# DMA transposes of x in two parts: a fused attention and MLP kernel

## The chip, the cores and the metric

One core of a Trainium2 chip runs the whole kernel. The metric is the device time of one execution in microseconds; the time of a kernel is the median over its runs.

## The reference

Eight batches of eight heads attend from 576 queries to keys and values that are averaged over groups of 8 positions (72 pooled positions). The heads are put side by side, which gives x with 4608 tokens (8 batches of 576) and 512 columns. Two matrix products with a pointwise function between them follow:

```
k_p = k.reshape(B, H, 72, 8, 64).mean(axis=3);  v_p likewise
attn = softmax(q @ k_p.T / 8);  x = (attn @ v_p), heads side by side
h = x @ w_in            # 4608 x 512 by 512 x 2048
g = h - tanh(h)
out = g @ w_out         # 4608 x 2048 by 2048 x 512
```

## The kernel before

All orders are written out by hand; no scheduler moves anything. Tokens are worked in nine groups of 512 (`TG`), while attention makes x in batches of 576 (`S`). Batch b starts at token 576 b and group g at 512 g, so a batch runs ahead of its group: batch g + 1, made during group g, holds tokens for group g + 1 and, more of them from batch to batch, for group g + 2. A batch comes in five blocks: four of 128 tokens and one of 64.

A start-up part makes batch 0, batch 1 and the first group. From then on each group g (loop at L931, g = 1 to 8) has two phases:

- The input phase: `h_pair` and `h_one` multiply xT, the transposed x, by w_in (`h_mms`, L530), ACT makes the tanh (L542), DVE subtracts (L543) into Gt. Among these stand the preparations for batch g + 1 and g + 2: `k_dma_transpose` (L332) turns the pooled keys kd into kT by a DMA, `k_place` on GpSimd puts them where the scores read them, `store_tile` (L607) stores the previous group's output, ACT casts the raw queries to q_bf in three parts (`q_cast_part`, L192 and L197), `q_dma_transpose` (L205) turns them into qT in five blocks, and then the raw k, v and q of batch g + 2 are loaded (L137, L146, L141, L170, L162).
- The output phase: the product with w_out, done by a Strassen scheme in two by two blocks, seven products in 14 half steps u (`product`, L586). Between the half steps stand the scores of batch g + 1 (u = 0 to 4, L349) and its five blocks of the product with v (`av`, at u = 6, 7, 8, 9 and 11, L396). DVE divides each block by its sum (L413, L414) into an x_sb tile, of which there are five, one for each block in turn. At u = 6 GpSimd begins to pool the keys and values of batch g + 2 (`pool_k`, `pool_v`; the pooled keys kd are done with L256).

`av` ends each block, from g = 1 on, with a DMA transpose (L434), which writes the block's columns into xT, a ring of three groups' tokens (`RING` = 1536). A block that crosses the ring's end is turned in two pieces, which is the case of block 1 of batch 5.

All DMA transposes and all loads of the loop are issued by SP, one after the other in program order. The stores of the loop are issued by GpSimd. For each group the order on SP is: kT, five qT, seven loads, then the five blocks of x.

Of the kernel before, what the change touches and what calls it, by code (L numbers as in the profile page):

```python
# [15 lines left out]
B, H, S, D = 8, 8, 576, 64  # L16
# [10 lines left out]
TG = 512  # L27
# [7 lines left out]
RING = 3 * TG  # L35
# [7 lines left out]
def kernel(  # L43
# [9 lines left out]
    nc = tc.nc  # L53
# [44 lines left out]
    xT = const.tile([128, NFB, RING], BF16, name="xT")  # L98
# [51 lines left out]
    def load_k(b):  # L150
        return [
            load_main(k_pairs, k_raw[b % 2], b, 0, NM),
            load_dense(k_pairs, k_raw[b % 2], b),
        ]

    def load_v(b):
        return [load_main(v_pairs, v_raw[b % 2], b, 0, NM)] + load_left(
            v_pairs, v_raw[b % 2], b
        )
# [29 lines left out]
    def q_cast_part(b, n):  # L189
        t = q_raws[b]  # L190
        if n < 2:
            nc.scalar.copy(  # L192
                out=q_bf[:, 2 * n : 2 * n + 2, :, :].rearrange("p j h d -> p h j d"),
                in_=t[:, :, 2 * n : 2 * n + 2, :],
            )
        else:
            nc.scalar.copy(out=q_bf[:QT, R, :, :], in_=q_raws.pop(b)[:QT, :, R, :])  # L197

    def q_dma_transpose(b, j0=0, j1=R + 1):
        if j0 == 0:  # L200
            qTs[b] = work.tile([128, NHP, S], BF16, name="qT", tag="qT")
        qT = qTs[b]
        for j in range(j0, j1):
            rows = 128 if j < R else QT
            nc.sync.dma_start_transpose(  # L205
                out=qT[:, :, j * 128 : j * 128 + rows],
                in_=q_bf[:rows, j, :, :].rearrange("p h d -> p (h d)"),
            )
# [121 lines left out]
    def k_dma_transpose(b):  # L330
        kT = work.tile([128, NT, 128], BF16, name="kT", tag="kT", bufs=1)
        nc.sync.dma_start_transpose(  # L332
            out=kT[:, :, :], in_=kdups.pop(b)[:, :, :, :].rearrange("p t a d -> p (t a d)")
        )
        kTs[b] = kT

    def k_place(b, eng):
        kT = kTs.pop(b)
        kb_main(KB[b % 2], kT[:, 0:NM, :], 0, NM, (eng, eng))
        kb_left(KB[b % 2], kT[:, NM, :], eng)  # L340
# [68 lines left out]
    def av_half(b, blk, half, x_sb, alloc):  # L409
        ps = alloc([128, 4, D1], FP32, "x_ps")  # L410
        av_mms(b, blk, half, ps)
        rden = work.tile([128, 4, 1], FP32, name="rden", tag="rden", bufs=4)
        nc.vector.reciprocal(out=rden[:, :, :], in_=ps[:, :, D:D1])  # L413
        nc.vector.tensor_tensor(  # L414
            out=x_sb[:, half, :, :],
            in0=ps[:, :, 0:D],
            in1=rden[:, :, :].to_broadcast([128, 4, D]),
            op=ALU.mult,
        )

    def new_x():
        return work.tile([128, 2, 4, D], BF16, name="x_sb", tag="x_sb", bufs=5)

    def av(b, blk, alloc, by_dma):
        x_sb = new_x()
        for half in range(2):
            av_half(b, blk, half, x_sb, alloc)
        if by_dma:
            p0 = 0 if blk < 4 else 64
            pos = (b * S + blk * 128) % RING  # L430
            p1 = min(128, p0 + RING - pos)
            for r0, r1, c in ((p0, p1, pos), (p1, 128, 0)):
                if r1 > r0:
                    nc.sync.dma_start_transpose(  # L434
                        out=xT[:, :, c : c + r1 - r0],
                        in_=x_sb[r0:r1, :, :, :].rearrange("p a h d -> p (a h d)"),
                    )
        return x_sb

    def x_pe_transpose(b, blk, x_sb, fbs=(0, 4)):  # L440
        p0 = 0 if blk < 4 else 64
        pos = b * S + blk * 128
        f0, f1 = fbs
        xf = x_sb.rearrange("p a h d -> p (a h d)")
        ps = ps_any([128, f1 - f0, 128], FP32, "xT_ps")
        for fb in range(f0, f1):
            nc.tensor.matmul(
                ps[:, fb - f0, p0:128],
                lhsT=xf[:, fb * 128 : (fb + 1) * 128],
                rhs=ident[:, p0:128],  # L450
                start=True,
                stop=True,
            )
        nc.scalar.copy(out=xT[:, f0:f1, pos : pos + 128 - p0], in_=ps[:, :, p0:128])
# [83 lines left out]
    def h_pair(g, p, b0, ts):  # L538
        h_mms(g, p, PS[:, b0, :])
        h_mms(g, p + NP, PS[:, b0 + 1, :])  # L540
        t2 = TS[:, 2 * ts : 2 * ts + 2, :]
        nc.scalar.activation(out=t2, in_=PS[:, b0 : b0 + 2, :], func=ACT.Tanh)  # L542
        nc.vector.tensor_sub(out=Gt[:, p, :, :], in0=PS[:, b0 : b0 + 2, :], in1=t2)  # L543

    def h_one(g, p, s, b0, ts):
        h_mms(g, p + s * NP, PS[:, b0, :])
        nc.scalar.activation(out=TS[:, ts, :], in_=PS[:, b0, :], func=ACT.Tanh)
        nc.vector.tensor_sub(out=Gt[:, p, s, :], in0=PS[:, b0, :], in1=TS[:, ts, :])  # L548

    def sum_p(a, b):  # L550
        nc.vector.tensor_tensor(  # L551
            out=P[:, a:b, :], in0=Gt[:, a:b, 0, :], in1=Gt[:, a:b, 1, :], op=ALU.add
        )

    def sum_q(a, b):
        nc.vector.tensor_tensor(
            out=Q[:, a:b, :], in0=Gt[:, a:b, 0, 0:HT], in1=Gt[:, a:b, 1, HT:TG], op=ALU.add
        )
# [9 lines left out]
    def w_sum(out, a, b, op, eng=nc.vector, k0=0, k1=NP):  # L568
        return eng.tensor_tensor(  # L569
            out=out[:, k0:k1, :], in0=a[:, k0:k1, :], in1=b[:, k0:k1, :], op=op  # L570
        )
# [33 lines left out]
    def store_tile(g, tb):  # L605
        for r0, r1, dst in out_segments(g * TG + tb * 128, 128):
            nc.gpsimd.dma_start(out=dst, in_=O[r0:r1, tb, :])  # L607
# [102 lines left out]
    for m, base, step, cm in (  # L710
# [6 lines left out]
            out=m,  # L717
            in_=m,
# [6 lines left out]
    for i in range(2):  # L725
# [4 lines left out]
        out=spread.rearrange("p (t x) -> p t x", x=32)[:, :, 0:LO],  # L730
        in_=ident[:, 0 : NM * LO].rearrange("p (x t) -> p t x", t=NM),
# [156 lines left out]
    for u in range(16):  # L888
# [28 lines left out]
        if u in (9, 11):  # L917
            n = (u - 9) // 2
            nc.scalar.mul(
                out=w2s[:, 4, 4 * n : 4 * n + 4, :], in_=b22[:, 4 * n : 4 * n + 4, :], mul=-1.0  # L920
# [10 lines left out]
    for g in range(1, NG):  # L931
        nb = g + 1 if g + 1 < B else None
        nn = g + 2 if g + 2 < B else None
        for p in range(NP - 1):
            c = p if g > 1 else p - 1
            if nb is not None and 0 <= c < 3:
                q_cast_part(nb, c)
            h_pair(g, p, (0, 2, 4, 6, 0, 2, 4)[p], p % 2)
            if g == 1 and p < 4:
                w_sum(w2s[:, 0, :, :], b11, b22, ALU.add, k0=2 * p, k1=2 * p + 2)  # L940
            if 3 <= p < 6:
                sum_p(2 * p - 6, 2 * p - 4)
            if nb is not None and p == 0:
                k_dma_transpose(nb)
                k_place(nb, nc.gpsimd.tensor_copy)
            if g > 1 and p == 0:
                for tb in range(4):
                    store_tile(g - 1, tb)
            if nb is not None and 0 <= c < 3:
                q_dma_transpose(nb, 2 * c, min(2 * c + 2, R + 1))  # L950
            if nb is not None and c == 2:
                if nn is not None:
                    load_k(nn)
                    load_v(nn)
                    load_q(nn)
        h_one(g, NP - 1, 1, 0, 2)
        h_one(g, NP - 1, 0, 1, 3)
        sum_p(6, 8)
        sum_q(0, 4)
        sum_q(4, 8)  # L960
        ps_a = Banks(2, 3, 4, 5, 0, 1)
        for u in range(14):
            n, half = u // 2, u % 2
            bk, lhs, rhs = products[n]
            if n == 6 and g == NG - 1:
                break
            product(g, bk, lhs, rhs, 4 * half, 4 * half + 4, n < 2)
            if half:
                after_product(g, n)
                if g == 1 and n in (1, 2):  # L970
                    w_sum(w2s[:, 2, :, :], b21, b22, ALU.add, k0=4 * n - 4, k1=4 * n)
            if nb is not None:
                if u < NT:
                    scores(nb, u)
                if u == NT:
                    ps_a.n += 2
                if u in (6, 7, 8, 9, 11):
                    av(nb, (6, 7, 8, 9, 11).index(u), ps_b1, True)
                if u == 6 and nn is not None:
                    pool_k(nn, nc.gpsimd)  # L980
                    pool_v(nn, nc.gpsimd)
        if g < NG - 1:
            nc.scalar.copy(out=O[:, 0:2, 0:HD], in_=chain(g, C1))  # L983
# [43 lines left out]
```

## Time and profile before

| what | value |
|---|---|
| runs, us | 298.24, 305.23, 305.66, 307.6, 300.93 |
| median, us | 305.23 |
| profiled execution, us | 298.24, of which the span 296.5 |
| PE, DVE, ACT, POOL busy | 94%, 77%, 52%, 49% of the span |
| DMA queue of SP and its share of the 16 engines' time | 54,736 packets, 35.6 MB, 50.2% |
| chain that ended last | PE 67%, DMA 16%, DVE 6%, POOL 4% |
| xT transposes | 31, landing 2.7 us after issue (median), 6.4 us at most |
| loads of k, v, q (1 MB each) | 9.1, 11.1 and 11.3 us from issue to landing |

The span is the time from the first to the last instruction of the profiled execution; the run's own time is 1.7 us longer. In the timeline, times are microseconds from the span's start. Group g's input phase starts at 55.97 (g = 1), 87.19, 117.17, 147.08, 176.57, 205.79, 235.46 and 261.54 (g = 8). On SP a line's duration is the time that the issue takes, not the transfer; the landing is told separately.

### The profile page before, as it was taken

How to read it: one execution, taken by the hardware profiler on the slowest of the kernel's cores; microseconds unless marked ns; L12 is line 12 of the kernel's file. 1: busy time of each engine (PE TensorE's matmuls, PEld its weight loads, DVE VectorE, ACT ScalarE, POOL GpSimd, SP SyncE). 2: the span in 40 equal slices, each digit the busy share in tenths (PEclk: the TensorE clock that was granted, in tenths of full speed). 3: DMA queues.
4: the chain of work that ended last, by engine and by line, in shares of the span. 5: the costliest groups of instructions: out<-in, count | busy, mean ns of one | idle time of the engine just before them, and what ended most of it. 6: DMA issues, size and time to landing. Idle time of an engine off the chain costs nothing.

```text
span 296.5 us, 5447 instructions
## 1 busy us (share of the span) xinstructions
PE 279.5 (94%) x2021; PEld 178.6 (60%) x2040; DVE 227.3 (77%) x400; ACT 153.8 (52%) x244; POOL 145.0 (49%) x166
## 2 busy tenths in 40 slices
PE   7899989999989999999999999999999999999980
PEld 2454445445864587458745874588458845854870
DVE  5658675799986987598859895989698769838940
ACT  4647586586327642764276527652765155136310
POOL 8500819970399439923993299329931040130020
PEclk9999999999999999999999999999999999999996
DMA  7999999938734999599949995999460450030014
GB/s 255 221 213 280 316 217 316 282 78 290 192 71 86 252 332 141 99 228 328 146 86 246 308 149 100 268 328 122 76 180 2 80 142 2 0 130 13 0 30 114
DMA packets 64587, 49.85 MB, mean 168 GB/s; under 512 B 39984, under 2 KB 53296, under 8 KB 64560
## 3 DMA queue, kind: packets, MB, share of 16 engines
q1 hardware_dynamic: 54736, 35.60, 50.2%
q0 software_dynamic: 7248, 12.06, 18.6%
q10 hardware_dynamic: 2576, 1.84, 2.2%
q8 instruction: 16, 0.26, 0.4%
q14 instruction: 11, 0.09, 0.1%
HBM read 36.70 MB, written 9.44 MB: 156 GB/s over the span
## 4 chain that ended last, share of the span: by engine, by line
PE 67%; DMA 16%; DVE 6%; POOL 4%; SPq 2%; issue 1%; ACT 1%; ACTq 0%; POOLq 0%
PE PS L530 30%; PE PS L586 26%; DMA w1b<-in_moe_w_in_dram 4%; PE PS L512 4%; DMA k_raw<-in_k_dram 4%; DMA xT<-x_sb 3%; PE PS L396 3%; DMA v_raw<-in_v_dram 3%; PE PS L349 3%; DVE Gt L543 3%; DMA qT<-q_bf 2%; POOL k_raw L248 1%; SPq L137 1%; DVE w2s L569 1%; ACT TS L542 1%
## 5 line engine op out<-in xcount | busy, mean ns | idle before, releaser
L530 PE MATMUL PS<-xT,w1b 128*128 128x512 bf16 x496 | 111.1, 379 | 3.5 <-DMA xT<-x_sb 1.8
L543 DVE TENSOR_TENSOR Gt<-PS,TS 128x1024 bf16<-128x1024 f32 x56 | 68.4, 1221 | 29.2 <-ACT TS L542 29.2
L530 PEld LDWEIGHTS <-w1b 128*128 128x128 f16 x512 | 49.7, 98 | 62.6 <-issue 2.2
L542 ACT ACTIVATE TS<-PS 128x1024 f32<-128x1024 f32 x56 | 57.4, 1025 | 33.1 <-PE PS L530 27.7
L631 POOL TENSOR_TENSOR m<-O,m 128x512 f32<-128x512 f32 x8 | 11.5, 1435 | 95.7 <-ACT m L630 64.9
L414 DVE TENSOR_TENSOR x_sb<-PS,rden 128x256 bf16<-128x256 f32 x72 | 30.6, 425 | 2.5
L586 PE MATMUL PS<-w2s,Dg 128*128 128x256 f16 x256 | 30.2, 272 | 0.0
L607 POOL DMA_DIRECT2D out_dram<-O x44 | 23.6, 546 | 13.4 <-ACT O L983 13.4
L248 POOL TENSOR_TENSOR k_raw<-k_raw 128x512 f32<-128x512 f32 (+2 forms) x13 | 21.6, 1675 | 17.0 <-DMA k_raw<-in_k_dram 17.0
L586 PEld LDWEIGHTS <-Gt 128*128 128x128 bf16 x256 | 24.5, 98 | 5.9 <-DVE Gt L548 0.5
L586 PEld LDWEIGHTS <-P 128*128 128x128 bf16 x256 | 24.6, 98 | 4.7 <-issue 1.4
L586 PEld LDWEIGHTS <-Dg 128*128 128x128 bf16 x256 | 24.6, 98 | 2.8 <-issue 0.2
L368 ACT ACTIVATE E<-PS 128x288 bf16<-128x288 f32 x60 | 21.4, 410 | 7.9 <-PE PS L349 7.8
L551 DVE TENSOR_TENSOR P<-Gt 128x1024 bf16<-128x1024 bf16 x32 | 22.0, 687 | 0.6
L561 DVE TENSOR_TENSOR Dg<-Gt 128x1024 bf16<-128x1024 bf16 x32 | 21.1, 717 | 0.0
L396 PE MATMUL PS<-VB,E 128*128 128x130 bf16 x240 | 20.2, 220 | 0.1
L637 ACT COPY m<-PS 128x512 f32<-128x512 f32 x8 | 4.7, 586 | 29.5 <-PE PS L586 29.5
L267 POOL TENSOR_TENSOR v_raw<-v_raw 128x512 f32<-128x512 f32 (+1 forms) x12 | 19.2, 1620 | 0.0
L396 PEld LDWEIGHTS <-E 128*128 128x128 bf16 x240 | 16.8, 98 | 1.9 <-issue 0.4
L349 PE MATMUL PS<-qT,KB 128*128 128x288 bf16 (+5 forms) x128 | 17.3, 289 | 0.5 <-DMA qT<-q_bf 0.3
L586 PE MATMUL PS<-w2s,Gt 128*128 128x256 f16 x128 | 16.7, 273 | 0.4 <-DVE Gt L548 0.2
L983 ACT COPY O<-PS 128x512 f32<-128x512 f32 x7 | 4.1, 586 | 24.5 <-PE PS L586 24.5
(109 smaller groups left out, 399.1 us busy)
## 6 DMA issues: line engine op xcount, KB each, us to landing
k_raw<-in_k_dram SPq DMA_DIRECT2D x7, 1024.0 KB, 9.1
q_raw<-in_q_dram SPq DMA_DIRECT2D x7, 1024.0 KB, 11.3
v_raw<-in_v_dram SPq DMA_DIRECT2D x7, 1024.0 KB, 11.1
out_dram<-O POOLq DMA_DIRECT2D x32, 128.0 KB, 3.9
out_dram<-O POOLq DMA_DIRECT2D x12, 256.0 KB, 3.7
w1b<-in_moe_w_in_dram POOLq DMA_DIRECT2D x4, 512.0 KB, 14.1
w2b<-in_moe_w_out_dram POOLq DMA_DIRECT2D x4, 512.0 KB, 16.6
out_dram<-O SPq DMA_DIRECT2D x4, 256.0 KB, 4.2
```

The lines of the kernel that those rows point to most:

```text
L248: first = eng.tensor_tensor(out=r[:, ta:tb, 0:4, :], in0=r[:, ta:tb, 0:4, :], in1=r[:, ta:tb, 4:8, :], op=ALU.add)
L349: nc.tensor.matmul(dst[p : p + w], lhsT=KB[b % 2][:, o : o + w], rhs=qTs[b][:, m, c0:c1], start=True, stop=True,)
L368: nc.scalar.activation(out=E[:, t, half * hs : (half + 1) * hs], in_=ps[:, :], func=ACT.Exp, scale=SCALE)
L396: nc.tensor.matmul(ps[:, 2 * n : 2 * n + 2, :].rearrange("p h d -> p (h d)") if n < 2 else ps.rearrange("p (a s) d -> p a s d", s=2)[:, :, ...
L414: nc.vector.tensor_tensor(out=x_sb[:, half, :, :], in0=ps[:, :, 0:D], in1=rden[:, :, :].to_broadcast([128, 4, D]), op=ALU.mult,)
L530: nc.tensor.matmul(dst, lhsT=w1b[:, fb, i * 128 : (i + 1) * 128], rhs=xT[:, fb, c0 : c0 + TG], start=(fb == 0), stop=(fb == NFB - 1),)
L542: nc.scalar.activation(out=t2, in_=PS[:, b0 : b0 + 2, :], func=ACT.Tanh)
L543: nc.vector.tensor_sub(out=Gt[:, p, :, :], in0=PS[:, b0 : b0 + 2, :], in1=t2)
L551: nc.vector.tensor_tensor(out=P[:, a:b, :], in0=Gt[:, a:b, 0, :], in1=Gt[:, a:b, 1, :], op=ALU.add)
L561: nc.vector.tensor_tensor(out=Dg[:, a:b, :, :], in0=Gt[:, a:b, :, 0:HT], in1=Gt[:, a:b, :, HT:TG], op=ALU.subtract,)
L586: nc.tensor.matmul(part(g, bk, tt), lhsT=lhs(k, slice(tt * 128, (tt + 1) * 128)), rhs=rhs[:, k, :], start=(first and k == 0 and (tt == 0 o ...
L607: nc.gpsimd.dma_start(out=dst, in_=O[r0:r1, tb, :])
```

## The change

The blocks of batch b that group b does not read (first token at or after 512 (b + 1)) are no longer turned by `av`. They are put on a list, and the list is emptied in the next group, at the begin of its output phase, ahead of the products. In SP's order, these transposes then stand behind the next group's kT, qT and loads, and ahead of that group's own blocks of x. For batches 2 and 3 these are blocks 3 and 4, for batches 4 and 5 blocks 2 to 4, for batches 6 and 7 blocks 1 to 4.

```diff
         if by_dma:
-            p0 = 0 if blk < 4 else 64
-            pos = (b * S + blk * 128) % RING
-            p1 = min(128, p0 + RING - pos)
-            for r0, r1, c in ((p0, p1, pos), (p1, 128, 0)):
-                if r1 > r0:
-                    nc.sync.dma_start_transpose(
-                        out=xT[:, :, c : c + r1 - r0],
-                        in_=x_sb[r0:r1, :, :, :].rearrange("p a h d -> p (a h d)"),
-                    )
+            if b * S + blk * 128 < (b + 1) * TG:
+                x_dma_transpose(b, blk, x_sb)
+            else:
+                late.append((b, blk, x_sb))
         return x_sb
+
+    late = []
+
+    def x_dma_transpose(b, blk, x_sb):
+        p0 = 0 if blk < 4 else 64
+        pos = (b * S + blk * 128) % RING
+        p1 = min(128, p0 + RING - pos)
+        for r0, r1, c in ((p0, p1, pos), (p1, 128, 0)):
+            if r1 > r0:
+                nc.sync.dma_start_transpose(
+                    out=xT[:, :, c : c + r1 - r0],
+                    in_=x_sb[r0:r1, :, :, :].rearrange("p a h d -> p (a h d)"),
+                )
...
         sum_p(6, 8)
         sum_q(0, 4)
         sum_q(4, 8)
+        while late:
+            x_dma_transpose(*late.pop(0))
         ps_a = Banks(2, 3, 4, 5, 0, 1)
```

## The prediction

> **What bounds the kernel now.** I read the page first, then busy times by group, the waits of PE and its weight loads, and the timeline of SP's queue. The profiled run took 298.24 us (span 296.5 plus 1.7 around it), the lowest of the five shown; their median is 305.23. About 2% of it, 6.1 us, is what a measurement of this kernel can tell from no change, so the bounds are 299.1 and 311.3.
>
> ```profile
> span 296.5 us, 5447 instructions
> PE 279.5 (94%) x2021; PEld 178.6 (60%) x2040; DVE 227.3 (77%) x400; ACT 153.8 (52%) x244; POOL 145.0 (49%) x166
> ```
>
> ```profile
> core 0: us, PE busy (x) PEld busy (x) DVE busy (x) ACT busy (x) POOL busy (x), PEclk, DMA share, GB/s
> 87.19:117.17 29.98, 29.45 (x220) 19.72 (x223) 24.63 (x48) 15.88 (x26) 20.22 (x23) 1.00 0.86 200
> 117.17:147.08 29.91, 29.27 (x220) 19.72 (x223) 24.12 (x41) 16.45 (x28) 18.79 (x20) 1.00 0.95 199
> 147.08:176.57 29.49, 29.27 (x220) 19.71 (x223) 24.43 (x43) 15.91 (x27) 18.85 (x22) 1.00 0.96 202
> ```
>
> These are groups 2, 3 and 4. PE is busy for 29.3 of 29.5 to 30.0 us at full clock, and the DMA engines for 0.86 to 0.96: two loops of nearly one length, PE's own and that of the loads.
>
> ```profile
> PE PS L530 <- DMA xT<-x_sb: 1.8, 3, 0.8
> PE PS L349 <- DMA qT<-q_bf: 0.3, 1, 0.3
> ```
>
> So transfers cost PE 2.1 us once the start is over: at the begin of groups 2, 3 and 4 (0.85, 0.41, 0.53) and in group 6's scores (0.28). SP's queue between two groups shows why:
>
> ```profile
> 140.20 8.80 SPq L434 DMA_TRANSPOSE xT<-x_sb  x5
> 149.10 1.23 SPq L332 DMA_TRANSPOSE kT<-kd  x1
> 150.43 6.60 SPq L205 DMA_TRANSPOSE qT<-q_bf  x5
> 157.09 1.54 SPq L137 DMA_DIRECT2D k_raw<-in_k_dram  x1
> ...
> 163.06 0.52 SPq L170 DMA_DIRECT2D q_raw<-in_q_dram  x1
> 166.58 0.63 SPq L162 DMA_DIRECT2D q_raw<-in_q_dram  x1
> 170.11 2.86 SPq L434 DMA_TRANSPOSE xT<-x_sb  x2
> ```
>
> Start, duration, line: SP works strictly in order. Turns of x for batch 4, then kT and qT of batch 5, then the loads for batch 6 from 157.09; the landing query gives 174.2 for the q load issued at 163.06 (11.1 us), and x blocks 0 and 1 land only behind it, at 176.1 and 176.4. PE's last product ends at 176.46.
>
> **What the change does to the queue.** Per batch, blocks 3 and 4 (batches 2, 3), 2 to 4 (4, 5) or 1 to 4 (6, 7) are moved: 18 of 30 blocks. No instruction is added. A turn holds SP 1.2 us and lands 2.45 us after issue when nothing is ahead of it. The moved ones no longer stand ahead of kT, qT and the loads of their own batch boundary; they stand behind the next loads and ahead of the next group's early blocks.
>
> *Taken away.* In the boundary shown, blocks 2 to 4 leave, so SP is free from 143.1. The next owner is then late for kT: its data.
>
> ```profile
> 144.55 1.86 POOL L256 TENSOR_TENSOR kd<-k_raw 128x640 bf16<-128x640 f32 x1
> ```
>
> kT can go at 146.4 instead of 149.10. q_bf's first part comes from ACT at 148.1 (L192, 147.07 + 1.05), its second at 151.0 and its tail at 152.4, so the five qT go at 148.2, 149.4, 151.1, 152.3 and 153.6, not 150.43 to 155.67, and the loads start at 155.0 instead of 157.09: 2.1 us ahead. The same working gives 3.3 for group 2, 1.25 for group 3 (kd only at 117.03, cast at 121.1) and 2.4 for group 5. Group 6 has no loads; its last qT goes at about 212.7 instead of 216.44 and lands before the score that waits at 220.8. Nothing holds the loads back otherwise: q_raw's last reader is the tail cast, the other buffers alternate.
>
> *Added behind the loads.* SP lets eight DMAs be open, which the order of waits in the built program gives: each waits for the one eight places before it. So the first moved block waits for k's small load, the second for v's main load, the rest for v's pieces just after. With loads 2.0 ahead in group 4, v lands at 168.4; moved blocks go at 165.3, 168.4 and 169.6, early block 0 at 170.8 (170.11 before) and block 1 at 172.0, in two pieces, the first landing by 174.5. That is 2 us before PE asks. If the loads do not land earlier (v 170.38), block 1 goes at 174.05 and lands at 176.5: 0.1 late. What needs care: the group that follows this output phase also reads the moved blocks. They come first in the queue, so block 1 still ends last. In group 5 only block 0 is early; groups 2 and 3 have two moved blocks each, done before the early blocks' x_sb.
>
> *A new wait.* x_sb has five buffers, so batch 5's block 2 is written over batch 4's block 2, now still to be turned behind the q load.
>
> ```profile
> 171.90 0.42 DVE L414 TENSOR_TENSOR x_sb<-PS,rden 128x256 bf16<-128x256 f32 x1
> 172.45 0.42 DVE L414 TENSOR_TENSOR x_sb<-PS,rden 128x256 bf16<-128x256 f32 x1
> ```
>
> The q load lands at 174.16, or at 172.1 with the head start; the turn some 0.5 after it (blocks 0 and 1 landed 0.3 apart). DVE stands for 0.8 us, or 2.8 without the head start. Queued behind are L638, blocks 3 and 4, L640; PE's pair 1 needs block 3's banks at 178.3 and DVE frees them at 176.0, so up to 2.3 us cost nothing. I take 0; the other end is 0.5 in each of groups 4 and 5.
>
> The moved turns of batch 4 could be issued from 143 on and are read from 176.57 on; in the new order they land at about 173, which leaves some 3 us of margin, and the row of 140.20 shows that a turn behind loads can take 6.4 us to land, not 2.45. The Trainium skill (DMA: Bandwidth & Descriptors, "Rules for kernel authors") advises to issue a DMA early and to wait for it late, which speaks against the change: by that rule alone the move brings nothing or a loss (305 or more). By the rows the margin holds, and the freed queue is what counts.
>
> **The sum.** On the profiled run the waits at the begin of group 3 (0.41), group 4 (0.53) and in group 6 (0.28) go: 1.2 us, 297.0. The 0.85 at group 2 stays: block 2's x_sb came from DVE at 84.48, its turn was issued at 84.69. Bounds: a gain of 2.1 (all waits), a loss of 1.1 (DVE's 0.5 twice, 0.1).
>
> The median is 7.0 above that run, and the profile doesn't show where. The chain has two sorts of transfer that nothing covers: at the start w1b 13.04 and k_raw 10.85, together 23.9 us, and the loads of groups 2, 3 and 4, first issue to q's landing 16.3, 18.1 and 17.1, together 51.5. In group 5 block 0 landed 1.5 ahead of PE, which takes up its share. If 7.0 lies on these 75.4 us (9.3%), the start has 2.2 and the groups 1.5, 1.7 and 1.6. The head starts then give back 1.5 + 0.41 in group 2 (of 3.3), 1.25 in group 3 (all that there is), 1.6 in group 4 (of 2.1) and 0.28 in group 6: 5.0 us. The forecast is 305.23 - 5.0 = 300.2. Ends: 303.9 if none of the excess is in the loads, 298.2 if all 7.0 come back.
>
> **Rivals.**
> 1. *All is recovered.* PE's own loop sets every run: 297.0. For it: 29.3 us of PE work in each group, and a head start above each wait but one. Against: group 3's 1.25, and the start, which no moved turn touches.
> 2. *The turns were hidden anyway.* The excess of the other runs is elsewhere; 305.23 - 1.2 = 304.0. For it: x blocks 3 and 4 were never waited for, and only 2.1 us of PE waits are there.
> 3. *The moved turns hold up the early ones (slower).* One turn issued under the q load, at 112.31, held SP 2.15 us, not 1.2. If all behind loads do so and the loads land no earlier, group 2 has late block 4, then blocks 0, 1, 2 from 110.3 on, the last landing at 119.2 against 117.04: 2.2 lost; group 4 has two moved ones and blocks 0 and 1 from 170.4 on, landing at 178.4: 1.9; group 5 loses 0.6; DVE's wait adds 1.0. With 5.7 more the median is 310.9, and with loads 9.3% longer, v landing 1 us later in three groups, 313. It decides once the q load lands less than about 1 us earlier than before. Against: three turns at 140.20 to 143.19 under the same load took 1.2 each.
>
> **How the numbers follow.** Forecast (300.2, own range 298.2 to 303.9) 0.46, of which 0.2 is under 299.1; all recovered 0.19; hidden anyway 0.19; held up 0.16, nearly all of it over 311.3. So faster 0.39, within 2% 0.46, slower 0.15. The range 296.4 to 306.0 holds all but the last, and little more than a tenth of hidden anyway's upper side.
>
> **What would show it.** Right: kT within 0.3 us of kd's end in groups 3 to 6, k loads 1.2 to 3.3 us earlier in their groups, the PE waits on xT down to group 2's 0.85, DVE waiting for a DMA at L414 in groups 4 and 5 only, under 2.3 us. Wrong: loads that start earlier but land at the old time (the DMA engines, not SP, then set them), turns of more than 2 us on SP, or PE at a group's begin waiting for longer than 0.5.

## The result, and the profile after

The changed kernel takes 299.88 us (median of 53 runs, 297.71 to 304.32); before it was 302.27 us in a larger sample (95 runs). The ratio is 0.9963, 95% interval 0.9948 to 0.9978: faster by about 0.4%, within the 2% that the forecast took as its bound. The ratio leaves out the runs of either kernel that are over 1.5% above its fastest, of which there are more before, and so shows less than the two medians do (0.992). The profiled execution took 300.18 us (span 298.4). The one shown before was the lowest of all runs of before, so a second profile of before (span 299.4, the first experiment) is set beside it.

The page of the changed kernel, its first lines, then groups 2 to 4 (begins at 87.69, 119.08, 148.50 and, for group 5, 179.07; columns as before):

```profile
span 298.4 us, 5451 instructions
PE 279.1 (94%) x2021; PEld 178.6 (60%) x2040; DVE 228.3 (76%) x400; ACT 153.7 (52%) x244; POOL 145.4 (49%) x166
```

```profile
87.69:119.08 31.39, 29.28 (x220) 19.72 (x223) 26.05 (x48) 17.02 (x27) 21.80 (x24) 1.00 0.88 191
119.08:148.50 29.42, 29.27 (x221) 19.72 (x224) 23.76 (x40) 14.79 (x25) 17.02 (x19) 1.00 0.93 198
148.50:179.07 30.57, 29.27 (x220) 19.70 (x223) 24.12 (x47) 17.48 (x28) 20.44 (x22) 1.00 0.82 195
```

PE's work is the same 29.3 us in each group. Group 3 is hardly longer than that work; groups 2 and 4 are, by 2.1 and 1.3 us. The waits of PE say by what (lines from L446 on have moved by 8; L538 is the old L530):

```profile
PE PS L538 <- DMA xT<-x_sb: 4.1, 3, 2.0
```

The wait for xT has grown from 1.8 to 4.1 us (3.0 in the second profile of before), with 2.0 at the begin of group 3 and 1.2 at that of group 5. The wait for qT is gone. SP's queue from the end of group 3 to that of group 4 (start, issue time, line; a turn is a DMA transpose, and the loads of one group are nine DMAs, two for k, five for v and two for q):

```profile
148.35 1.20 SPq L332 DMA_TRANSPOSE kT<-kd  x1
150.05 6.42 SPq L205 DMA_TRANSPOSE qT<-q_bf  x5
156.52 0.58 SPq L137 DMA_DIRECT2D k_raw<-in_k_dram  x1
...
161.07 0.54 SPq L170 DMA_DIRECT2D q_raw<-in_q_dram  x1
163.52 2.84 SPq L162 DMA_DIRECT2D q_raw<-in_q_dram  x1
166.46 12.14 SPq L443 DMA_TRANSPOSE xT<-x_sb  x6
```

kT goes 0.02 us after kd's end (148.33) and the k load 8.0 us after the group's begin, not 10.0. But the six turns of x, three moved ones and then blocks 0 and 1 (block 1 in two pieces), take 12.14 us of SP, where six took 8.81 before. The line of the first of them alone (minimum, median and maximum of its issue time in ns):

```profile
L443 SPq DMA_TRANSPOSE xT<-x_sb x1: 4486/4486/4486, 166.5 to 166.5; - x1
```

And DVE in the same stretch, with the idle time before an instruction and what ended it:

```profile
167.49 0.69 DVE L634 TENSOR_TENSOR O<-PS,m 128x512 f32<-128x512 f32 x1 [1.15 <-DMA out_dram<-O]
...
175.19 0.42 DVE L414 TENSOR_TENSOR x_sb<-PS,rden 128x256 bf16<-128x256 f32 x1 [1.57 <-DMA xT<-x_sb]
```

The second wait was forecast. The first was not: DVE may not write rows 2 and 3 of O (L634, the old L626) before the previous group's stores have read them.

### The profile page after: what moved, and what is told of

Read it like the earlier page. It is cut to its first block, busy times and chain, and to the rows that moved or that the text cites. A ratio compares the mean times of both kernels' runs of the same rounds, so it can differ in the third digit from the quotient of the medians.

```text
span 298.4 us, 5451 instructions
## 1 busy us (share of the span) xinstructions
PE 279.1 (94%) x2021; PEld 178.6 (60%) x2040; DVE 228.3 (76%) x400; ACT 153.7 (52%) x244; POOL 145.4 (49%) x166
## 4 chain that ended last, share of the span: by engine, by line
PE 64%; DMA 17%; POOL 8%; DVE 6%; issue 1%; ACT 1%; ACTq 0%; SPq 0%; POOLq 0%; DVEq 0%
PE PS L538 28%; PE PS L594 25%; DMA xT<-x_sb 7%; DMA w1b<-in_moe_w_in_dram 4%; PE PS L520 4%; DMA k_raw<-in_k_dram 4%; PE PS L396 3%; DVE Gt L551 3%; PE PS L349 3%; DMA out_dram<-O 2%; DVE w2s L577 1%; POOL out_dram L615 1%; POOL v_raw L267 1%; POOL k_raw L248 1%; DVE P L559 1%
## 5 line engine op out<-in xcount | busy, mean ns | idle before, releaser
L538 PE MATMUL PS<-xT,w1b 128*128 128x512 bf16 x496 | 111.1, 379 | 6.2 <-DMA xT<-x_sb 4.1
L538 PEld LDWEIGHTS <-w1b 128*128 128x128 f16 x512 | 49.7, 98 | 65.3 <-issue 4.8
L414 DVE TENSOR_TENSOR x_sb<-PS,rden 128x256 bf16<-128x256 f32 x72 | 30.6, 425 | 5.9 <-DMA xT<-x_sb 3.6
L594 PEld LDWEIGHTS <-Gt 128*128 128x128 bf16 x256 | 24.5, 98 | 5.8 <-DVE Gt L556 0.5
L594 PEld LDWEIGHTS <-P 128*128 128x128 bf16 x256 | 24.6, 98 | 4.7 <-issue 1.4
L594 PEld LDWEIGHTS <-Dg 128*128 128x128 bf16 x256 | 24.6, 98 | 2.6
L569 DVE TENSOR_TENSOR Dg<-Gt 128x1024 bf16<-128x1024 bf16 x32 | 23.2, 784 | 0.0
L993 ACT COPY O<-PS 128x512 f32<-128x512 f32 x7 | 4.1, 586 | 24.5 <-PE PS L594 24.5
```

Of the source, the lines that this page charges most:

```text
L414: nc.vector.tensor_tensor(out=x_sb[:, half, :, :], in0=ps[:, :, 0:D], in1=rden[:, :, :].to_broadcast([128, 4, D]), op=ALU.mult,)
L538: nc.tensor.matmul(dst, lhsT=w1b[:, fb, i * 128 : (i + 1) * 128], rhs=xT[:, fb, c0 : c0 + TG], start=(fb == 0), stop=(fb == NFB - 1),)
L569: nc.vector.tensor_tensor(out=Dg[:, a:b, :, :], in0=Gt[:, a:b, :, 0:HT], in1=Gt[:, a:b, :, HT:TG], op=ALU.subtract,)
L594: nc.tensor.matmul(part(g, bk, tt), lhsT=lhs(k, slice(tt * 128, (tt + 1) * 128)), rhs=rhs[:, k, :], start=(first and k == 0 and (tt == 0 o ...
```

## Experiments

The ratios below are to the kernel before, measured on the same chip.

**1. The kernel before, once more.**

> The unchanged kernel, for a second profile of it: the one shown before was the lowest of its runs (298.24 against a median of 302.27). If the excess of the other runs lies in the loads of groups 2 to 5, as the forecast had it, this profile is 2 to 5 us longer, PE waits for xT at the begins of groups 3 to 6 for more than 3 us in all, and the part before group 1 is within 0.5 us of 55.97. If the excess lies elsewhere, the waits for xT stay at 1 to 2 us and the extra time is spread over the start or over PE's own work. The ratio to the kernel before is 1.00 within 0.4% in either case.

303.01 us, ratio 1.0024 (0.9984 to 1.0064). Its waits of PE, and its groups 2 to 4:

```profile
PE PS L530 <- DMA xT<-x_sb: 3.0, 3, 1.1
PE PS L349 <- DMA qT<-q_bf: 2.3, 2, 1.3
```

```profile
86.88:118.05 31.17, 29.45 (x221) 19.69 (x223) 25.06 (x46) 15.87 (x26) 20.12 (x23) 1.00 0.86 192
118.05:149.65 31.60, 29.45 (x220) 19.63 (x223) 25.58 (x46) 17.24 (x28) 19.09 (x21) 1.00 0.94 191
149.65:180.10 30.45, 29.27 (x220) 19.70 (x223) 24.77 (x44) 16.29 (x27) 19.24 (x22) 1.00 0.87 194
```

Against the first profile these groups are longer by 1.2, 1.7 and 1.0 us, 3.8 in all, and the start is not (56.01 against 55.97). So the excess of this run, 301.14 us against 298.24, does lie in the loops of the loads. A part of it that the first profile hardly showed (0.3) is the wait for qT: the last qT of group 3, issued at 126.86 among the stores and loads, landed 7.1 us later, and PE stood in the scores.

**2. The stores of rows 2 and 3 first.**

```diff
-                for tb in range(4):
+                for tb in (2, 3, 0, 1):
                     store_tile(g - 1, tb)
```

> The changed kernel with the four stores of a group in the order 2, 3, 0, 1. Theory A: the loads start earlier as forecast (1.3 to 2.8 us), but this pushes the stores behind them; DVE's first write into rows 2 and 3 of O waits for the stores (1.5 and 1.2 us in groups 2 and 4 of the changed kernel's profile), the x_sb come later and with them the turns. Then those waits are gone here, the begin of group 3 comes 1 to 2 us earlier, and the time is 298.5 (ratio 0.988). Theory B: all 16 DMA engines are busy from the first store to the last turn, so the landing of q sets the begin of the group whatever DVE does: 299.9 (ratio 0.992 to 0.996).

298.23 us, ratio 0.9884 (0.9835 to 0.9932). Group 3 begins 29.9 us after group 2 and not 31.4. The waits of DVE:

```profile
DVE x_sb L414 <- DMA xT<-x_sb: 3.3, 3, 2.3
DVE rden L413 <- PE PS L396: 2.6, 7, 0.4
```

No wait for the stores is among them any more; in the changed kernel it was 2.6 us. Theory A is right on this step: the wait at O was on the path, above all in group 2. At the begin of group 5 nothing is gained: that group begins 30.7 us after group 4, against 30.6 in the changed kernel.

**3. Seven x_sb buffers.**

```diff
-        return work.tile([128, 2, 4, D], BF16, name="x_sb", tag="x_sb", bufs=5)
+        return work.tile([128, 2, 4, D], BF16, name="x_sb", tag="x_sb", bufs=7)
...
-            kdups[b] = work.tile([128, NT, 2, D], BF16, name="kd", tag="kd")
+            kdups[b] = work.tile([128, NT, 2, D], BF16, name="kd", tag="kd", bufs=1)
```

> The changed kernel with seven x_sb buffers in place of five, and one kd buffer in place of two to make room: a moved block is then not written over before its turn. Both theories: the waits of DVE for a DMA ahead of x_sb (1.6 and 1.8 us in groups 4 and 5) are gone. As forecast they cost PE nothing, since PE needs the banks 2.3 us later: 299.9, ratio to the changed kernel 1.00. If they were on the path after all: 1 us less, 298.9.

300.30 us, ratio 0.9959 (0.9921 to 0.9997), as the changed kernel. DVE no longer waits for a turn at x_sb (the only wait for a DMA that the list still names is 1.4 us at O), and nothing is gained: the forecast's 0 for this wait holds.

**4. The moved turns ahead of the loads.**

```diff
+            if (c == 2 or nb is None) and p >= 2:
+                while late:
+                    x_dma_transpose(*late.pop(0))
             if nb is not None and c == 2:
...
-        while late:
-            x_dma_transpose(*late.pop(0))
         ps_a = Banks(2, 3, 4, 5, 0, 1)
```

> The moved turns stand between the last qT and the loads of the next group, so kT and qT keep their head start and the loads lose it (two to four turns of 1.2 us). Nothing stands behind the loads but the early blocks. Theory A (the head start of the loads is what gains, and the turns behind the loads give part of it back): loads start 10 to 11 us after the begin of the group as before, no turn holds SP for more than 2.5 us, no DVE wait at x_sb or O; 301 to 302, ratio 0.998 to 1.00. Theory C (the gain comes from kT and qT being early): 299.9 or less, ratio 0.992.

302.22 us, ratio 1.0021 (0.9986 to 1.0055): no gain. The loads start 10.9 and 11.6 us after the begin in groups 2 and 3, 13.8 and 14.8 in groups 4 and 5, where three turns stand ahead. That is later than before the change (10.0 and 10.3 in groups 4 and 5), which the expectation did not see. PE waits, in the profile of the longest of its twelve runs:

```profile
PE PS L538 <- DMA xT<-x_sb: 5.5, 3, 3.6
```

kT and qT are early here too, and PE doesn't wait for qT. That theory C's 0.992 did not come fits theory A, but since the loads are not only without their head start but late, this run can't tell what early kT and qT are worth by themselves.

**5. Both edits, 2 and 3.**

> The changed kernel with both edits: seven x_sb buffers and the stores of rows 2 and 3 first. With the store order alone DVE still waited 2.3 us at x_sb in group 4, and PE 1.3 us for the bank that DVE then freed late at the begin of group 5. Theory A (each of the two waits was on the path, and each hid the other): neither wait is left, no group begins more than 0.6 us late but group 2 (0.86), and the time is 297.0 (ratio 0.984). Theory B (the landing of q sets the begin of the group): the wait for xT takes the place of the DVE wait in group 5, and the time stays at 298.2 (ratio 0.988).

298.80 us, ratio 0.9903 (0.9867 to 0.9939): no better than the store order alone, so theory B holds here and theory A falls. PE waits 1.2 us at the begin of group 3 and 1.5 at that of group 5, where block 1 of x landed at 177.62, though DVE waited for no DMA. The list puts the 1.5 down to DVE (L414), which ended an x_sb at 177.66. But PE began 0.25 us after the landing, as it did in the changed kernel (178.83 and 179.07), where no x_sb ended in between, so the turn is the likelier cause. In run 2 too PE began 0.25 us after that landing (177.01), so the 1.3 us that the expectation puts down to a bank are likelier the turn's. What is left is then the transfer itself, behind the loads.

**6. The store order in the kernel before.**

> The kernel before the change with only the store order 2, 3, 0, 1. If the wait at O is made by the change (loads that start earlier push the stores behind them), there is nothing to gain here: ratio 1.00, no DVE wait for a DMA, waits for xT and for qT as in the second profile of before (3.0 and 2.3 us). If the store order were good by itself: ratio 0.99 or less.

301.69 us, ratio 0.999 (0.9951 to 1.0029); PE waits 2.9 us for xT and 2.6 for qT. Without the change the edit gains nothing that can be measured. The change did not make the wait at O out of nothing, though. The first profile of before has it in group 2, under ACT's name:

```profile
106.24 0.69 DVE L626 TENSOR_TENSOR O<-PS,m 128x512 f32<-128x512 f32 x1 [1.20 <-ACT E L368]
```

The last store had landed at 106.06. In the changed kernel the same write of group 2 began 0.18 us after the last landing as well (106.84 and 107.02), after 1.48 us of idle time; in groups 4 and 5 before, where the stores had landed over 2 us ahead of the write, the idle time was about 0.45. So the change made a wait longer in group 2 that could be there before (run 8, unchanged in that group, has it too: landing 106.25, write 106.43), and added one of 1.15 us in group 4.

**7. The q load from ACT, with both edits.**

```diff
                     load_k(nn)
+                    load_q(nn, False, nc.scalar)
                     load_v(nn)
-                    load_q(nn)
+                    load_q_tail(nn, q_raws[nn], nc.sync)
```

> On top of seven x_sb buffers and stores 2, 3 first, the q load is issued by ACT, ahead of the v load in program order and 5.3 us after the begin of the group, so it starts some 2.5 us ahead of the k load and is not ahead of the turns in SP's rings. Theory A (turns wait because they stand behind q on one queue, and SP is held until older DMAs land): turns of x land within 3 us of issue or with v's landing, the moved turn's issue no longer takes over 3 us once v is in, DVE and PE waits for xT are gone but for group 2's 0.86, 296.0 to 297.0. Theory B (the DMA engines' total work sets it): loads of k and v land later by what q takes first, the turns land at the same time, 297 to 298.5. A third way: qT lands late because it shares the engines with q (over 6 us), PE waits in the scores, 300.

296.77 us, ratio 0.9835 (0.9793 to 0.9877), theory A. (`nc.scalar` is ACT, `nc.sync` SP.) In group 4 q starts 5.4 us after the begin, ahead of the stores (8.2) and the k load (8.3), and v's main load is in after 22.4 us instead of 22.0 in the changed kernel, but nothing large stands behind it: the moved turns take 1.3, 2.0 and 1.2 us of SP, and x blocks 0 and 1 land 27.1 and 27.5 us after the begin, 1.8 ahead of PE.

```profile
PE PS L538 <- DMA xT<-x_sb: 0.8, 1, 0.8
```

That is group 2's wait, set by DVE, which no edit touched. Groups 2 to 6 take 29.2 to 29.3 us each: PE's own work. The edit moves q to another queue and also 7 us forward; which of the two gains was not tried apart.

**8. Batches 6 and 7 alone.**

```diff
-            if b * S + blk * 128 < (b + 1) * TG:
+            if b < 6 or b * S + blk * 128 < (b + 1) * TG:
```

> Only the blocks of batches 6 and 7 are moved, where no loads follow; batches 2 to 5 as before. By the forecast this part is worth 0.28 us (the last qT of group 6 lands ahead of the score): ratio 0.999 to 1.00. If the gain of the change were mostly here: ratio 0.996.

302.82 us, ratio 0.9976 (0.993 to 1.0022). The interval holds the forecast's 0.999 to 1.00 and 0.996 as well; this run doesn't decide.

**9. The q load from ACT in the kernel before.**

> The kernel before the change, with the q load issued by ACT ahead of the v load. Theory A (turns wait because q stands ahead of them in SP's rings, and the engines stand idle before the loads start): q uses the idle time from 5 us after the begin of the group, v lands 3 us earlier than before, waits for xT go but for group 2; the last qT stand among q and the stores, and PE's wait for qT stays or grows (2 to 4 us): 298 to 301, ratio 0.985 to 0.995. If the moved turns were needed for any gain: 302, ratio 1.00.

310.91 us, ratio 1.0284 (1.0222 to 1.0346): both expectations missed. Theory A's half sentence was right in kind and far off in size:

```profile
PE PS L349 <- DMA qT<-q_bf: 10.2, 5, 3.9
PE PS L530 <- DMA xT<-x_sb: 0.8, 1, 0.8
```

The waits for xT are gone but for group 2's, but measured from the begin the qT of group 3 go 2.3 to 3.1 us later than those of run 7's group 4, among the q load and the stores, and the last four of group 3 land 8.1 to 9.9 us after issue.

**10 and 11. The q load from ACT in the changed kernel, without and with the store order.**

> The changed kernel, with the q load issued by ACT ahead of the v load, five x_sb buffers and the stores in the old order. Theory A: with the loads in 3 us earlier the turns no longer hold SP and x_sb is free in time, so that neither more buffers nor the store order is needed for that: DVE's wait at x_sb gone; the stores land no earlier than 18 us after the begin of the group, so DVE may still wait at O for about 1 us, which the earlier turns cover: 296.8, as with all three edits. If the two other edits each carried part of the gain: 298.

> The changed kernel with the q load from ACT and the stores of rows 2 and 3 first, five x_sb buffers. By theory A 296.8, no wait of DVE for a DMA over 0.5 us. It is the candidate for a version that beats both kernels with the fewest edits.

298.81 us, ratio 0.9831 (0.9755 to 0.9908), and 296.33 us, ratio 0.9784 (0.9732 to 0.9837). In both profiles no wait for xT is left but the 0.8 of group 2, and groups 3 to 5 begin without a wait for a turn. But run 10's profile still has the wait at O, in group 3, and again the list names ACT for it:

```profile
136.23 0.69 DVE L634 TENSOR_TENSOR O<-PS,m 128x512 f32<-128x512 f32 x1 [2.28 <-ACT E L368]
```

The last store landed at 136.10. Measured from the begin the write is 1.8 us later than in run 11, the x_sb follow it, PE waits for DVE four times behind it (1.1 us in the list), and the group takes 31.1 us instead of 29.2. The expectation had this wait covered by earlier turns; in this profile it isn't. Whether the store order adds something to the time once q is off SP's queue stays open, since the intervals overlap. Run 11 beats both kernels, by 2.2% and, through the ratios to before, by some 1.8%. The q load needs the moved turns: without them it costs 2.8% (run 9), with them alone the ratio is 0.9831 (run 10).

## Why the prediction was right or wrong

- **The queue.** Right. The k load starts 8.3, 7.8, 8.0 and 7.8 us after the begins of groups 2 to 5, before 11.1, 9.1, 10.0 and 10.3: 2.8, 1.3, 2.0 and 2.5 ahead, forecast 3.3, 1.25, 2.1 and 2.4. kT goes 0.03 us after kd's end in groups 2, 4 and 6, 0.13 in group 3 and 0.43 in group 5 (forecast: 0.3 at most).
- **What the head start is worth.** This step failed. The forecast carried it undiminished to q's landing and from there to PE. Measured from the begin, q lands 25.2, 25.6, 25.6 and 25.5 us later, before 27.4, 27.2, 27.1 and 26.8: 2.2, 1.6, 1.5 and 1.3 us, against head starts of 2.8, 1.3, 2.0 and 2.5. The last turn that PE needs then lands 31.3 us (group 2), 29.3 (3) and 30.3 (4) after the begin, before 29.9, 29.8 and 29.4. Only group 3 keeps a gain. Against the second profile of before it is the same (31.0, 31.5 and 30.3), though against that one q lands 4.0 and 3.0 us earlier in groups 2 and 3.
- **The moved turns behind the loads.** Mis-sized: 1.2 us of SP each, in the forecast; the first one in each of groups 2 to 5 took 4.0, 3.4, 4.5 and 4.3. Rival 3's mechanism is real, with a larger term than its 2.15. In groups 3 and 5 the early blocks had the slack for it. In group 4 it decided: block 1's x_sb was ready 25.0 us after the begin, but its turn was issued only at 26.8, when SP was through with the moved ones, and landed at 30.3 (before: ready and issued at 24.7, landed at 29.4). Rival 3's own sum is a little low: with its 2.15 us for block 0 too, group 4 would lose 2.8 us, not 1.9.
- **A wait that was left out.** The forecast has no term for DVE's wait at O. With loads that start earlier, the stores are pushed back: in group 4 they land 18.9 us after the begin, before 16.0, and in group 2 19.2, before 18.9 and 17.1 in the two profiles. DVE then waits 1.5 us in group 2 and 1.2 in group 4, and in group 2 the x_sb of the early blocks come 1.2 to 1.4 us later than in the first profile of before; in group 4 it is 0.3 at most. Of the former the write itself has 0.3; the four sums behind it took 3.56 us instead of 2.49, for a reason that was not tried. In the second profile of before the x_sb of group 2 come within 0.1 us as late (24.5, 26.2 and 27.3 us after the begin, here 24.6, 26.3 and 27.4), there because PE had waited for qT: the wait at O took the place of that one. Taking the wait away brought about as much again as the change gained: ratio 0.9884 instead of 0.9963, or 298.23 us instead of 299.88. The same edit brought nothing without the change (run 6).
- **The wait at x_sb.** Right: 1.6 and 1.8 us, groups 4 and 5, no cost (run 3, and run 5 against run 2). A wait of 0.2 in group 2 was not forecast.
- **The wait for qT.** 0.28 us in the forecast, from the lowest run; 2.3 us in an ordinary one, and gone with the change. This term was too small, and it offsets part of the loss above.
- **The excess of ordinary runs.** The groups' part was about right (1.5, 1.7 and 1.6 forecast; 1.2, 1.7 and 1.0 in run 1), the start's 2.2 wrong (0.04). That the sizes fit is partly luck: they were worked out for a run 7.0 us above the lowest, and run 1's profile is 2.9 above it.
- **The sum.** 5.0 us were forecast; the ratio gives 1.1 (0.0037 of 302.27) and the medians 2.4. The forecast time of 300.2 came close to 299.88 by luck: the five runs that it stood on had a median 3.0 us above that of the larger sample, and the gain was overstated by nearly as much. Two of the signs that the forecast itself named for being wrong are there: turns of more than 2 us on SP, and PE waiting for longer than 0.5 us at a group's begin (2.0 and 1.2).
- **The advice against it.** The Trainium skill's rule to issue early and wait late (DMA: Bandwidth & Descriptors, "Rules for kernel authors") was read in the forecast as "nothing or a loss". That reading doesn't hold here: the ratio's interval, 0.9948 to 0.9978, lies wholly below 1. The moved turns did pay for standing behind the loads (3.4 to 4.5 us of SP each for the first), but what had stood behind them gained more.
- **The rivals.** Rival 2 (hidden anyway) named the size that the ratio shows, 1.2 us, but not the reason: runs 1 and 2 show a gain and a loss of about 2 us each (the wait for qT, the wait at O) that offset one another. Rival 1's time of 297.0 was reached only with further edits, in runs 7 and 11 (296.77 and 296.33).

## What to carry to other kernels

When a transfer is moved out of one place in an in-order queue, ask not only who goes earlier but what it now stands behind, and what the earlier transfer pushes back on the same engines: here the head start came as computed, and the long issues behind the loads and a longer wait for the stores took most of it. Moving a large load off the queue of the small urgent transfers can pay, but here only with those of the same stage ahead of it: the q load from ACT gave 1.3% on top of the moved turns (0.9963 to 0.9831) and cost 2.8% without them. When a wait list names an engine that had no part in the data, look at what landed just before: twice here it was a store. A lowest run hides what ordinary runs lose; take the waits from a second profile before pricing them.

## What the hardware showed that was not expected

A turn issued behind open loads held SP until older loads were coming in: the four long issues ended at 109.28, 141.24, 170.95 and 200.30, and pieces of the v load landed at 109.3, 141.3, 170.9 and 200.3. That looks like a limit on what may be queued, but that was not tried, and issues of 1.5 to 2.8 us elsewhere in these groups did not end with the v load. And a turn that lands 2.45 us after issue when it is alone took 8.1 to 9.9 us among a load from another queue and the stores (run 9).
